# Attention masks as 64-row products beside the scores they mask, in a fused attention, expert and convolution kernel

## The chip, the core and the metric

The kernel runs on one core of one Trainium2 chip. Time is device time in microseconds (us) of one execution; less is better. Before the change three runs took 479.0, 471.89 and 477.14 us, the median is 477.14 us. Names of engines: PE multiplies matrices, PEld is its weight load, DVE, ACT and POOL work element by element, SP issues the transfers.

## The reference

Three layers follow each other on a batch of 4. The first is attention with 8 heads of width 64 over 512 local and 32 global tokens; a local query sees the global keys and the local keys at most 32 positions away. The second has 4 experts, each a causal attention over the 544 tokens with a head width of 64, of which every token takes two by its gate. The third is a projection to 1024 channels, a convolution of width 3 along the tokens, a gate and a projection back.

```python
mask = np.abs(pos[:, None] - pos[None, :]) <= 32
s_ll = np.where(mask, scale * q_l @ k_l.T, -1e9)          # local attention
a_l = softmax(concat([scale * q_l @ k_g.T, s_ll]))
x = concat([softmax(scale * q_g @ k_all.T) @ v_all, a_l @ concat([v_g, v_l])])
for e in range(4):                                         # experts
    scores = np.where(causal, -1e9, scale * (x @ wq[e]) @ (x @ wk[e]).T)
    out += gate[e] * (softmax(scores) @ (x @ wv[e]) @ wo[e])
h = relu(out @ w_in)                                       # convolution and gate
y = (h * sigmoid(conv3(h))) @ w_out
```

## The kernel before

The program is recorded as a list of operations and put in order by a planner (class `Recorder`, lines 154 to 314): each operation has a due number, set by `due(...)`, and a cost by engine, and each engine takes the ready operation with the lowest due number whose tiles have a free buffer. The due numbers come from the table in lines 37 to 40. Every instruction is emitted in line 314, so the profile names all of them L314, and one tells them apart by the names of their tiles. A float32 product of full accuracy is made of three products of split operands (names ending in h and l).

Phase A (one batch, four pairs of heads; `phase_a`) computes local attention. `scores_l` takes two score tiles `s`, one for each head of a pair. Sixteen blocks of 32 queries by 128 keys go into each: block 4i + j lies on PSUM partitions 32j to 32j + 31. The two heads lie on the two halves of the partitions, so a score product (`s<-rk,rq`) uses 64 rows and 32 columns of PE's array. The mask is added by products too: for each head and each j the product of 32 columns of an identity (`identb`) with the table `lmask` (`s<-lmask,identb`, 512 columns wide, bfloat16), over all 128 rows. DVE then takes the maximum (`ml`), ACT the exponential (`Pa`). `scores_g` does the 32 global queries (`Pg`, `PGT`), `pv_l` and `pv_g` multiply with the values (`t<-vr,p` and `t<-PGT,vr`).

Phase B (`phase_b`) makes queries and keys of four experts (`s<-xh,wqkh` and the like), values (`s<-wvh,xh`) and the gates. For each of 2 pairs of experts and 4 blocks of 128 queries, `scores` runs six score products over 64 rows, three for each expert (`s<-kh,qh`, `s<-kl,qh`, `s<-kh,qlo`), the two experts on the two halves of the rows. Two products of the full identity with `causal` follow over all 128 rows (`s<-cm,identb`, 128 by 128). `trans` (`t<-ident,w`) and `pv` (`t<-p,vB`) use the result; `last` handles the last 32 queries.

Phase C (`phase_c`) multiplies with the folded weight (`s<-oh,wfh`), does the convolution on ACT and DVE, and multiplies with the output weight (`s<-gh,wuh`). The fold (`s<-gl,oh`), and the decoding of 64-bit weights on DVE and POOL that fold and output weight need, run in the first 200 us beside phases A and B of the first two batches.

SP loads in one queue in the planner's order: the mask tables (`w<-in_cmask_dram`), keys and queries (`rk`, `rq`), values (`vr`), weights.

Of the kernel before, what the change touches and what calls it, by code (L numbers as in the profile page):

```python
# [8 lines left out]
F32 = mybir.dt.float32  # L9
F32R = mybir.dt.float32r  # L10
BF = mybir.dt.bfloat16
I32 = mybir.dt.int32
# [11 lines left out]
BIG = 1e9  # L24
# [9 lines left out]

AHEAD = 1

PERIOD, A_AT, A_STEP, LOAD_AHEAD = 54.5, 0.0, 5.0, 21.5
B_AT, LAST, ITEMS, ITEM_STEP = 29.0, 54.0, 9.0, 2.45
C_AT, C_HALF, C_PROJ = 80.0, 41.0, 36.5
FOLD, FOLD_STEP, WOUT, WOUT_STEP = 12.0, 1.45, 75.0, 2.0  # L40


def local_mask():

    import numpy as np
    m = np.zeros((128, 4, 128), np.float32)
    q = np.arange(32)[:, None]
    for n in range(NG_):
        for c, kb in enumerate(KEYS[FIRST[n]:FIRST[n] + 4]):
            if kb != "g":  # L50
                t = 32 * kb + np.arange(32)[None, :]
                ok = (abs(q + 32 * n - t) <= 32) & (t >= 0) & (t < SL)
                m[32 * (n % 4):32 * (n % 4) + 32, n // 4, 32 * c:32 * c + 32] = np.where(ok, 0.0, -BIG)
    return m
# [282 lines left out]
def width(v):  # L337
    n = 1
    for k in v.shape[1:]:
        n *= k  # L340
    return n


def cost_pe(node, method, out, args, kw):
    us = 0.0 if node.calls else 0.03
    node.lag = 0.25
    if method == "transpose":
        return us + 0.11
    lhs, N = args[1], width(out)
    K, M = lhs.shape[0], width(lhs)  # L350
    if lhs.dt == F32R:
        one = max(0.107, N / 2400 + 0.013)
        return us + (one if K > 64 else one / 2)
    if lhs.dt == BF:
        return us + (0.06 if M == 32 else max(0.107, N / 2400 + 0.013))
    if K == 64:
        return us + max(0.03, N / 2400 if N > 128 else 0.0)
    if M == 32 and N == 64:
        return us + 0.03
    if N >= 256 or N == 64:  # L360
        return us + 4 * N / 2400 + 0.03
    return us + (0.066 if N <= 32 else 0.115)
# [24 lines left out]
def body(ctx, tc, kq, vA, w_gate, wqk, wv, woT, w_in, conv_w, w_out, cmask, out):  # L387
    nc = tc.nc
    NB = kq.shape[0]
    rec = Recorder()  # L390
    pe, act = rec.engine("PE", nc.tensor, cost_pe), rec.engine("ACT", nc.scalar, cost_act)
    dve, pool = rec.engine("DVE", nc.vector, cost_dve), rec.engine("POOL", nc.gpsimd, cost_pool)
    sp = rec.engine("SP", nc.sync, cost_dma)
# [4 lines left out]
    def T(shape, dt, name, bufs=1):  # L398
        return rec.tile(sb, shape, dt, name, bufs)

    def due(us):
        rec.due = us
# [7 lines left out]
    def W2():  # L410
        return T([128, 512], F32, "w2", 4)
# [52 lines left out]
    identb = T([128, 128], BF, "identb")  # L464
    dve.tensor_copy(identb, ident)

    cm = T([128, 160], BF, "cm")
    causal, last_mask = cm[:, :128], cm[:, 128:160]
    trif = T([128, 4, 4], F32, "trif")

    due(-30)
# [17 lines left out]
    def projections_gen():  # L489
        due(-5)  # L490
        w = W2()
        sp.dma_start(w[:, :160], cmask[:, 512:672])
        dve.tensor_copy(cm, w[:, :160])
        sp.dma_start(trif, cmask[:, 672:688].rearrange("p (a b) -> p a b", a=4))
        w = W2()
        pool.memset(w[:, :256], 0.0)
        for t in (ql, qll):
            scale_pool(t, w[:, :256].rearrange("p (a b) -> p a b", a=2), 1.0)
        for c in range(4):
            due(4 + 2 * c)  # L500
            w = W2()
            sp.dma_start(w, wqk[128 * c:128 * c + 128])
            split(wqkh[:, c], wqkl[:, c], w, act)
        for c in range(4):
            due(14 + 2 * c)
            w = W2()
            sp.dma_start(w[:, :256], wv[128 * c:128 * c + 128])
            sp.dma_start(w[:, 256:260], w_gate[128 * c:128 * c + 128])
            split(wvh[:, c], wvl[:, c], w[:, :260], act)
# [28 lines left out]

    def conv_load():
        due(FOLD)  # L540
        rawc = T([128, 24, 2], I32, "rawc")
        sp.dma_start(rawc.rearrange("p a b -> p (a b)"), conv_w.bitcast(I32))
        decode(rawc, 24, cw.rearrange("p k f -> p (k f)"))

# [10 lines left out]
    NPA, NPT = 2, 4  # L555
    NRK, NRQ, NXQ = 2, 2, 1
    xs = {}
    lmask = T([128, 512], BF, "lmask")


    Pg = T([128, 6, 128], F32, "Pg")
# [43 lines left out]
    def scores_l(k, q):  # L605

        t = [PS(4, 128) for _ in range(2)]
        rows = [slice(64 * y, 64 * y + 64) for y in range(2)]
        P = [T([128, 4, 128], F32, "Pa", NPA) for _ in range(2)]
        rec.claim(*P)  # L610
        with rec.group():
            for y in range(2):
                for j in range(4):
                    r = slice(32 * j, 32 * j + 32)
                    pe.matmul(t[y][r].rearrange("p i c -> p (i c)"), identb[:, r], lmask, start=True, stop=False)
            for i in range(4):
                for j in range(4):
                    g = 4 * i + j
                    for y in range(2):
                        pe.matmul(t[y][32 * j:32 * j + 32, i], q[rows[y], 32 * g:32 * g + 32],  # L620
                                  k[rows[y], 32 * FIRST[g]:32 * FIRST[g] + 128], start=False, stop=(i == 3))

        ml = T([128, 4, 4, 2], F32, "ml", 3)
        for y in range(2):
            dve.tensor_reduce(ml[:, 0, :, y], t[y], axis=AX.X, op=ALU.max, negate=True)
            dve.tensor_scalar(ml[:, 0, :, y], ml[:, 0, :, y], SCALE, None, op0=ALU.mult)
            for i in range(4):
                act.activation(P[y][:, i], t[y][:, i], AF.Exp, bias=ml[:, 0, i, y:y + 1], scale=SCALE,
                               accum_out=ml[:, 1, i, y:y + 1])
        dve.tensor_scalar(ml[:, 2], ml[:, 1], EPS, None, op0=ALU.add)  # L630
        dve.reciprocal(ml[:, 3], ml[:, 2])
        return P, ml[:, 3]
# [60 lines left out]

    def consts_a():
        due(-25)
        w = W2()
        sp.dma_start(w, cmask[:, :512])
        dve.tensor_copy(lmask, w)

    def phase_a(b):  # L700
        for c in range(0, 4, 2):
# [28 lines left out]
    def phase_b(b):  # L730
# [3 lines left out]
        for t, (dh, dl, sc) in enumerate(((qh, qlo, 0.125), (kh, kl, 1.0))):  # L734
            for p in range(2):
                m = slice(256 * t + 128 * p, 256 * t + 128 * p + 128)
# [15 lines left out]
        for i in range(5):  # L752
            r = 128 if i < 4 else 32
# [4 lines left out]
            with rec.group():  # L758
              for c in range(4):
                for xa, wa in ((xh, wvh), (xh, wvl), (xl, wvh)):  # L760
                    pe.matmul(acc[:r, :260], xa[c][:, 128 * i:128 * i + r], wa[:, c, :], start=(n == 0),
                              stop=(n == 11))
# [31 lines left out]
        for e in range(4):  # L794
            r0, p = 64 * (e % 2), e // 2
# [7 lines left out]
        for z in range(2):  # L803
            w = keys[z].stop - keys[z].start
            t = PS(512)[:, :w]
# [20 lines left out]
        t = PO(4, 128)  # L826
# [5 lines left out]
        t = PO(4, 128)  # L832
# [5 lines left out]
        def scores(p, i):  # L838

            st = T([128, 8], F32, "stB", 4)  # L840
            w = 128 * (i + 1)
            qi = slice(128 * i, 128 * i + 128)
            t = [PS(512) for _ in range(2)]
            PB = [W2() for _ in range(2)]
            rec.claim(*PB)
            with rec.group():
                for n, (a, k) in enumerate(((qh, kh), (qh, kl), (qlo, kh))):
                    for y in range(2):
                        rows = slice(64 * y, 64 * y + 64)
                        pe.matmul(t[y][:, :w], a[rows, p, qi], k[rows, p, :w], start=(n == 0), stop=False)  # L850
                for y in range(2):
                    pe.matmul(t[y][:, w - 128:w], identb, causal, start=False, stop=True)
            for y in range(2):
                dve.tensor_reduce(st[:, y:y + 1], t[y][:, :w], axis=AX.X, op=ALU.max, negate=True)
                P = PB[y]
                act.activation(P[:, :w], t[y][:, :w], AF.Exp, bias=st[:, y:y + 1],
                               accum_out=st[:, 2 + y:3 + y])
            dve.tensor_scalar(st[:, 4:6], st[:, 2:4], EPS, None, op0=ALU.add)
            dve.reciprocal(st[:, 4:6], st[:, 4:6])
            for y in range(2):  # L860
                pool.tensor_scalar(PB[y][:, :w], PB[y][:, :w], st[:, 4 + y:5 + y],
                                   gate[:, i, 2 * p + y:2 * p + y + 1], op0=ALU.mult, op1=ALU.mult)
            live[p, i] = PB
# [132 lines left out]
def host_layout(inputs):  # L996
    import numpy as np
    c = np.ascontiguousarray
# [5 lines left out]
    for n in range(NG_):  # L1004
        for j, kb in enumerate(KEYS[FIRST[n]:FIRST[n] + 4]):
            for y in range(2):
                if kb == "g":
                    vA[:, :, 32 * j:32 * j + 32, n, y] = vg[:, y::2]
                elif 0 <= kb < NG_:
                    vA[:, :, 32 * j:32 * j + 32, n, y] = vl[:, y::2, 32 * kb:32 * kb + 32]  # L1010
    cm = np.zeros((128, 688), np.float32)
    cm[:, :512] = local_mask().reshape(128, 512)
    p = np.arange(128)
    cm[:, 512:640] = np.where(p[None, :] > p[:, None], -BIG, 0.0)
    cm[:, 640:672] = np.where(p[None, :32] > (p[:, None] % 32), -BIG, 0.0)
    cm[:, 672:688] = np.where(np.arange(4)[None, :] < np.arange(4)[:, None], 1.0, 0.0).reshape(1, 16)
    bits = lambda w: c(w).view(np.int64)
    hw = lambda w: np.concatenate(list(w), axis=1)

# [36 lines left out]
```

## Time and profile before

| | |
|---|---|
| Median of three runs | 477.14 us (471.89 to 479.0) |
| Profiled execution | 474.14 us, its span 472.3 us |
| PE busy | 440.8 us, 93% of the span |
| DVE, ACT, POOL busy | 72%, 65%, 36% |
| Read from memory | 38.40 MB |

Matmuls are pipelined: on this page a matmul of 272 columns shows 0.29 us of duration while the next one starts 0.125 us later. What one costs is therefore read as the distance between two starts, and a busy PE is not a PE at its peak. In a name such as `64*32 64x128` the first pair is rows and columns of the array in use, the second what streams through it.

### The profile page before, as it was taken

The numbers are of one execution on the slowest core, as the hardware profiler recorded it, in microseconds if no ns is written. First come the engines' busy times: TensorE is split into PE (matmuls) and PEld (weight loads), VectorE is DVE, ScalarE is ACT, GpSimd is POOL, SyncE is SP. The second block draws the span as 40 slices with busy tenths as digits, with TensorE's granted clock in tenths as the row PEclk, the third lists the DMA queues.
The fourth block names the chain that finished last, engine by engine and source line by source line (L and its number), as shares of the span: only waits on it lengthen the run. The fifth ranks groups of instructions, "written<-read, shape, count | busy, mean of one in ns | idle before, by whom it ended". The sixth has DMA issues, their size and how long they took to land.

```text
span 472.3 us, 14650 instructions
## 1 busy us (share of the span) xinstructions
PE 440.8 (93%) x5768; PEld 382.9 (81%) x5768; DVE 338.6 (72%) x970; ACT 305.8 (65%) x1017; POOL 168.9 (36%) x285
## 2 busy tenths in 40 slices
PE   5688799999989998999999999999999999999996
PEld 2556699765779886779879987799899997989996
DVE  3586677989987998899528746688448386957770
ACT  3677574667667776778448846586568454837771
POOL 2066879864786637950000011330000033400000
PEclk9989899999989999999999999999999999999999
DMA  8977612443561124320134004300100000000101
GB/s 291 303 239 257 218 46 81 145 152 122 171 214 47 44 72 159 96 98 15 58 129 147 14 7 154 104 14 14 63 21 3 0 26 25 13 26 1 48 25 47
DMA packets 21348, 43.79 MB, mean 93 GB/s; under 512 B 3104, under 2 KB 8352, under 8 KB 21280
## 3 DMA queue, kind: packets, MB, share of 16 engines
q1 hardware_dynamic: 21280, 42.86, 27.1%
q8 instruction: 45, 0.74, 0.7%
q14 instruction: 23, 0.19, 0.1%
HBM read 38.40 MB, written 4.46 MB: 91 GB/s over the span
## 4 chain that ended last, share of the span: by engine, by line
PE 59%; DVE 16%; POOL 9%; ACT 6%; issue 5%; DMA 3%; SPq 0%; DVEq 0%; POOLq 0%; ACTq 0%
PE s L314 43%; PE t L314 16%; DVE cv L314 6%; POOL cv L314 4%; POOL hb L314 3%; DVE hb L314 2%; DVE gl L314 2%; DVE stB L314 2%; DVE ml L314 2%; ACT cv L314 2%; DMA vr<-in_vA_dram 1%; ACT hb L314 1%; DMA w<-in_w_gate_dram 1%; POOL gl L314 1%; DMA rq<-in_kq_dram 1%
## 5 line engine op out<-in xcount | busy, mean ns | idle before, releaser
L314 PE MATMUL s<-gh,wuh 128*128 128x272 f32 x256 | 78.4, 306 | 0.4 <-ACT gh L314 0.3
L314 POOL TENSOR_SCALAR w<-w,stB,gate 128x128 f32<-128x128 f32 (+3 forms) x64 | 42.9, 681 | 91.5 <-DVE glast L314 44.2
L314 DVE SCALAR_TENSOR_TENSOR cv<-hb,cw,cv 128x272 f32<-128x272 f32 x128 | 64.4, 515 | 15.1 <-ACT cv L314 12.4
L314 PE MATMUL s<-gl,wuh 128*128 128x272 f32 x256 | 74.1, 289 | 0.6 <-DVE gl L314 0.5
L314 PE MATMUL s<-gh,wul 128*128 128x272 f32 x256 | 73.8, 288 | 0.0
L314 ACT ACTIVATE Pa<-s,ml 128x128 f32<-128x128 f32 x128 | 45.7, 368 | 29.4 <-DVE ml L314 25.8
L314 PEld LDWEIGHTS s<-gh,wuh 128*128 128x128 f32 x256 | 48.4, 189 | 2.2 <-ACT gh L314 1.1
L314 PEld LDWEIGHTS s<-gl,wuh 128*128 128x128 f32 x256 | 48.3, 189 | 1.3 <-DVE gl L314 1.3
L314 PEld LDWEIGHTS s<-gh,wul 128*128 128x128 f32 x256 | 48.3, 189 | 0.0
L314 ACT ACTIVATE w<-s,stB 128x128 f32<-128x128 f32 (+3 forms) x64 | 33.5, 527 | 16.4 <-DVE stB L314 16.0
L314 POOL TENSOR_SCALAR hb<-hb 128x256 f32<-128x256 f32 (+1 forms) x33 | 36.7, 1112 | 11.1 <-ACT hb L314 11.0
L314 PE MATMUL s<-oh,wfh 128*128 128x274 f32 x128 | 38.2, 299 | 1.2 <-DVE kl L314 0.8
L314 PE MATMUL s<-xh,wqkh 128*128 128x272 f32 x128 | 38.5, 301 | 0.0
L314 PE MATMUL s<-xh,wqkl 128*128 128x272 f32 x128 | 38.2, 299 | 0.0
L314 PE MATMUL s<-xl,wqkh 128*128 128x272 f32 x128 | 38.0, 297 | 0.0
L314 DVE COPY p<-t 128x128 f32<-128x128 f32 (+3 forms) x64 | 29.9, 484 | 10.9 <-PE t L314 10.8
L314 PE MATMUL s<-oh,wfl 128*128 128x274 f32 x128 | 37.2, 290 | 0.0
L314 PE MATMUL s<-ol,wfh 128*128 128x274 f32 x128 | 37.1, 290 | 0.0
L314 POOL TENSOR_TENSOR cv<-cv,hb 128x256 f32<-128x256 f32 (+1 forms) x33 | 25.1, 760 | 33.6 <-DVE hb L314 32.3
L314 ACT ACTIVATE cv<-cv 128x272 f32<-128x272 f32 x64 | 27.4, 429 | 13.5 <-DVE cv L314 12.7
L314 PE MATMUL t<-ident,w 128*128 128x128 f32 x176 | 30.3, 282 | 5.1 <-POOL w L314 2.7
L314 DVE TENSOR_REDUCE stB<-s 128x1 f32<-128x128 f32 (+3 forms) x64 | 29.8, 483 | 6.6 <-PE s L314 6.2
(152 smaller groups left out, 1257.3 us busy)
## 6 DMA issues: line engine op xcount, KB each, us to landing
vr<-in_vA_dram SPq DMA_DIRECT2D x32, 512.0 KB, 5.6
rk<-in_kq_dram SPq DMA_DIRECT2D x16, 384.0 KB, 3.8
rq<-in_kq_dram SPq DMA_DIRECT2D x16, 272.0 KB, 4.2
out_dram<-y SPq DMA_DIRECT2D x32, 136.0 KB, 1.7
w<-in_w_in_dram SPq DMA_DIRECT2D x16, 256.0 KB, 3.0
w<-in_w_out_dram SPq DMA_DIRECT2D x16, 256.0 KB, 2.6
w<-in_wqk_dram SPq DMA_DIRECT2D x4, 256.0 KB, 5.7
w<-in_woT_dram SPq DMA_DIRECT2D x2, 256.0 KB, 6.8
```

The lines of the kernel that those rows point to most:

```text
L314: getattr(n.eng.nc, method)(*map(real, args), **{k: real(v) for k, v in kw.items()})
```

## The change

The local mask goes through 64 rows. Its table is stored twice, once on each half of the partitions, as two pieces of 512 columns for queries 0 to 63 and 64 to 127 of a tile; each head uses the rows of its own half, the same array tile as its scores. There are still eight products of 512 columns.

The causal mask is cut in two as well. Each half of the mask's rows stands on both halves of the partitions. For each expert two products over its own 64 rows replace one over 128: the first takes the mask for queries 0 to 63 and is 128 columns wide, the second for queries 64 to 127 and is 64 wide. Where the query half is not the expert's own half of the partitions, the identity with swapped halves (`swapb`) takes the place of `identb`. Two products become four.

The constants grow from 688 to 1456 columns and are loaded in three pieces in place of two. `ml` has 2 buffers in place of 3, `rawc` shares the buffers of `w64`. The table of the planner's due numbers is new, so operations move on all engines.

```diff
-PERIOD, A_AT, A_STEP, LOAD_AHEAD = 54.5, 0.0, 5.0, 21.5
-B_AT, LAST, ITEMS, ITEM_STEP = 29.0, 54.0, 9.0, 2.45
...
+PERIOD, A_AT, A_STEP, LOAD_AHEAD = 54.0, 0.0, 6.0, 1.5
+B_AT, LAST, ITEMS, ITEM_STEP = 29.0, 54.0, 9.0, 2.35
...
-        return us + (0.06 if M == 32 else max(0.107, N / 2400 + 0.013))
+        return us + (0.06 if K == 64 else max(0.107, N / 2400 + 0.013))
...
-        sp.dma_start(w[:, :160], cmask[:, 512:672])
-        dve.tensor_copy(cm, w[:, :160])
...
+        sp.dma_start(w[:, :416], cmask[:, 1024:1440])
+        dve.tensor_copy(cm, w[:, :416])
...
-        rawc = T([128, 24, 2], I32, "rawc")
+        rawc = T([128, 512], F32, "w64", 2).bitcast(I32)[:, :48].rearrange("p (a b) -> p a b", b=2)
...
-                    pe.matmul(t[y][r].rearrange("p i c -> p (i c)"), identb[:, r], lmask, start=True, stop=False)
+                    one = 64 * y + 32 * (j % 2)
+                    pe.matmul(t[y][r].rearrange("p i c -> p (i c)"), identb[rows[y], one:one + 32],
+                              lmask[rows[y], j // 2], start=True, stop=False)
...
-        ml = T([128, 4, 4, 2], F32, "ml", 3)
+        ml = T([128, 4, 4, 2], F32, "ml", 2)
...
-        w = W2()
-        sp.dma_start(w, cmask[:, :512])
-        dve.tensor_copy(lmask, w)
+        for h in range(2):
+            w = W2()
+            sp.dma_start(w, cmask[:, 512 * h:512 * h + 512])
+            dve.tensor_copy(lmask[:, h], w)
...
-                for y in range(2):
-                    pe.matmul(t[y][:, w - 128:w], identb, causal, start=False, stop=True)
+
+                for h in range(2):
+                    for y in range(2):
+                        rows = slice(64 * y, 64 * y + 64)
+                        pe.matmul(t[y][:, w - 128 + 64 * h:w], (identb if h == y else swapb)[rows],
+                                  causal[rows, h, 64 * h:], start=False, stop=(h == 1))
...
+    twice = lambda m: np.stack([np.concatenate([h, h]) for h in (m[:64], m[64:])], axis=1).reshape(128, -1)
```

Two places show what moves. The first is the head of SP's queue. Before, the first keys and queries (`rk`, `rq`) stood behind one piece of constants:

```order
L314 DMA w_70<-in_cmask_dram 128x512
L314 DMA rk<-in_kq_dram 128x768
L314 DMA rq<-in_kq_dram 128x544
L314 DMA rk<-in_kq_dram 128x768
L314 DMA rq<-in_kq_dram 128x544
L314 DMA vr<-in_vA_dram 128x1024 x3
L314 DMA w_101<-in_cmask_dram 128x160
L314 DMA trif<-in_cmask_dram 128x16
```

Now:

```order
L314 DMA w_70<-in_cmask_dram 128x512
L314 DMA w_77<-in_cmask_dram 128x512
L314 DMA w_81<-in_cmask_dram 128x416
L314 DMA trif<-in_cmask_dram 128x16
L314 DMA rk<-in_kq_dram 128x768
L314 DMA rq<-in_kq_dram 128x544
L314 DMA rk<-in_kq_dram 128x768
L314 DMA rq<-in_kq_dram 128x544
```

All constants now stand ahead of the first keys.

The second is PE at the second item of the first batch's phase B: six score products and the causal mask behind them. Before:

```order
L314 MATMUL s<-kh,qh 128x128 x2
L314 MATMUL s<-kl,qh 128x128 x2
L314 MATMUL s<-kh,qlo 128x128 x2
L314 LDWEIGHTS identb
L314 MATMUL s<-cm,identb 128x128
L314 LDWEIGHTS identb
L314 MATMUL s<-cm,identb 128x128
L314 MATMUL s<-wvh,xh 32x260
```

The same kind of group now (`s<-cm` is the product with `swapb`, which lies in `cm`):

```order
L314 MATMUL s<-kh,qh 128x128 x2
L314 MATMUL s<-kl,qh 128x128 x2
L314 MATMUL s<-kh,qlo 128x128 x2
L314 LDWEIGHTS identb
L314 MATMUL s<-cm,identb 128x128
L314 LDWEIGHTS cm
L314 MATMUL s<-cm 128x128
L314 LDWEIGHTS cm
L314 MATMUL s<-cm 128x64
L314 LDWEIGHTS identb
L314 MATMUL s<-cm,identb 128x64
L314 MATMUL s<-oh,wfh 128x274
```

Four loads and four products stand where two and two stood.

## Rows read from the trace of the kernel before

**Rows 1.** The page, its head and part 1: busy time of each engine.

```profile
span 472.3 us, 14650 instructions
PE 440.8 (93%) x5768; PEld 382.9 (81%) x5768; DVE 338.6 (72%) x970; ACT 305.8 (65%) x1017; POOL 168.9 (36%) x285
```

**Rows 2.** Busy time by stretch; PEclk is the granted clock as a share.

```profile
core 0: us, PE busy (x) PEld busy (x) DVE busy (x) ACT busy (x) POOL busy (x), PEclk, DMA share, GB/s
0.00:60.00 60.00, 44.60 (x875) 32.06 (x876) 36.01 (x105) 37.00 (x135) 29.08 (x43) 0.94 0.77 258
60.00:200.00 140.00, 130.97 (x1891) 109.64 (x1889) 122.25 (x361) 95.38 (x336) 100.93 (x139) 0.99 0.34 113
200.00:450.00 250.00, 246.56 (x2865) 223.12 (x2864) 171.61 (x485) 163.01 (x522) 38.77 (x103) 1.00 0.14 46
450.00:472.30 22.30, 18.71 (x145) 18.07 (x143) 8.77 (x21) 10.38 (x27) 0.10 (x1) 1.00 0.11 38
```

**Rows 3.** Waits of PE from 60 us on, longest in total first.

```profile
PE t L314 <- POOL w L314: 2.7, 4, 1.5
PE s L314 <- POOL gl L314: 2.2, 4, 0.9
PE t L314 <- DVE ol L314: 2.0, 4, 0.7
```

**Rows 4.** Timeline of PE at a local mask: start, duration, operation.

```profile
194.24 0.44 PE L314 MATMUL t<-ident,w 128*128 128x128 f32 x2
194.61 0.61 PE L314 MATMUL s<-lmask,identb 128*32 128x512 bf16 x8
195.15 1.16 PE L314 MATMUL s<-rk,rq 64*32 64x128 f32 x64
196.24 0.33 PE L314 MATMUL t<-ident,w 128*128 128x128 f32 x1
```

**Rows 5.** Timeline of PE, a causal mask with a 128-row stage behind it.

```profile
207.15 0.39 PE L314 MATMUL s<-kl,qh 64*128 64x512 f32 x2
207.38 0.40 PE L314 MATMUL s<-kh,qlo 64*128 64x512 f32 x2
207.71 0.29 PE L314 MATMUL s<-cm,identb 128*128 128x128 bf16 x2
207.81 0.37 PE L314 MATMUL s<-oh,wfh 128*128 128x274 f32 x1
208.02 0.29 PE L314 MATMUL s<-ol,wfh 128*128 128x274 f32 x1
208.15 0.29 PE L314 MATMUL s<-oh,wfl 128*128 128x274 f32 x1
```

**Rows 6.** Timeline of PE, a causal mask with column tiles behind it.

```profile
393.00 0.34 PE L314 MATMUL s<-kl,qh 64*128 64x384 f32 x2
393.17 0.34 PE L314 MATMUL s<-kh,qlo 64*128 64x384 f32 x2
393.44 0.28 PE L314 MATMUL s<-cm,identb 128*128 128x128 bf16 x2
393.65 0.66 PE L314 MATMUL t<-p,vB 128*64 128x128 f32 x8
```

**Rows 7.** Timeline of PE, 64 small products of 128 rows, then 128x128.

```profile
294.75 1.17 PE L314 MATMUL t<-vr,p 128*32 128x64 f32 x64
295.86 0.39 PE L314 MATMUL s<-gh,wuh 128*128 128x272 f32 x1
296.08 0.29 PE L314 MATMUL s<-gl,wuh 128*128 128x272 f32 x1
```

**Rows 8.** Timeline of PE, 64-row pairs, then full products of 32 columns.

```profile
82.17 0.27 PE L314 MATMUL s<-kl,qh 64*128 64x128 f32 x2
82.28 0.27 PE L314 MATMUL s<-kh,qlo 64*128 64x128 f32 x2
...
211.08 0.26 PE L314 MATMUL s<-kh,qlast_l 128*128 128x32 f32 x1
211.19 0.26 PE L314 MATMUL s<-kh,qlast_h 128*128 128x32 f32 x1
```

**Rows 9.** Timelines of SP and PE at the start.

```profile
0.72 0.37 SPq L314 DMA_DIRECT2D w<-in_cmask_dram  x1
1.14 0.42 SPq L314 DMA_DIRECT2D rk<-in_kq_dram  x1
...
3.73 1.05 PE L314 MATMUL s<-lmask,identb 128*32 128x512 bf16 x8 [3.73 <-DVE lmask L314]
5.93 3.78 PE L314 MATMUL s<-rk,rq 64*32 64x128 f32 x80 [1.16 <-DMA rq<-in_kq_dram]
```

More of the change, by code (lines that the diff above doesn't have):

```diff
@@ L35 @@
 AHEAD = 1
-PERIOD, A_AT, A_STEP, LOAD_AHEAD = 54.5, 0.0, 5.0, 21.5
-B_AT, LAST, ITEMS, ITEM_STEP = 29.0, 54.0, 9.0, 2.45
-C_AT, C_HALF, C_PROJ = 80.0, 41.0, 36.5
-FOLD, FOLD_STEP, WOUT, WOUT_STEP = 12.0, 1.45, 75.0, 2.0
+PERIOD, A_AT, A_STEP, LOAD_AHEAD = 54.0, 0.0, 6.0, 1.5
+B_AT, LAST, ITEMS, ITEM_STEP = 29.0, 54.0, 9.0, 2.35
+C_AT, C_HALF, C_PROJ = 80.0, 42.0, 43.5
+FOLD, FOLD_STEP, WOUT, WOUT_STEP = 12.0, 1.25, 75.0, 2.0
 def local_mask():
@@ L465, in body @@
     dve.tensor_copy(identb, ident)
-    cm = T([128, 160], BF, "cm")
-    causal, last_mask = cm[:, :128], cm[:, 128:160]
+    cm = T([128, 416], BF, "cm")
+    causal, swapb, last_mask = cm[:, :256].rearrange("p (h k) -> p h k", h=2), cm[:, 256:384], cm[:, 384:416]
     trif = T([128, 4, 4], F32, "trif")
@@ L491, in projections_gen @@
         w = W2()
-        sp.dma_start(w[:, :160], cmask[:, 512:672])
-        dve.tensor_copy(cm, w[:, :160])
-        sp.dma_start(trif, cmask[:, 672:688].rearrange("p (a b) -> p a b", a=4))
+        sp.dma_start(w[:, :416], cmask[:, 1024:1440])
+        dve.tensor_copy(cm, w[:, :416])
+        sp.dma_start(trif, cmask[:, 1440:1456].rearrange("p (a b) -> p a b", a=4))
         w = W2()
@@ L557, in body @@
     xs = {}
-    lmask = T([128, 512], BF, "lmask")
+    lmask = T([128, 2, 512], BF, "lmask")
     Pg = T([128, 6, 128], F32, "Pg")
@@ L1010, in host_layout @@
                     vA[:, :, 32 * j:32 * j + 32, n, y] = vl[:, y::2, 32 * kb:32 * kb + 32]
-    cm = np.zeros((128, 688), np.float32)
-    cm[:, :512] = local_mask().reshape(128, 512)
+    twice = lambda m: np.stack([np.concatenate([h, h]) for h in (m[:64], m[64:])], axis=1).reshape(128, -1)
+    cm = np.zeros((128, 1456), np.float32)
+    cm[:, :1024] = twice(local_mask().reshape(128, 512))
     p = np.arange(128)
-    cm[:, 512:640] = np.where(p[None, :] > p[:, None], -BIG, 0.0)
-    cm[:, 640:672] = np.where(p[None, :32] > (p[:, None] % 32), -BIG, 0.0)
-    cm[:, 672:688] = np.where(np.arange(4)[None, :] < np.arange(4)[:, None], 1.0, 0.0).reshape(1, 16)
+    cm[:, 1024:1280] = twice(np.where(p[None, :] > p[:, None], -BIG, 0.0))
+    cm[:, 1280:1408] = np.where(p[None, :] == (p[:, None] + 64) % 128, 1.0, 0.0)
+    cm[:, 1408:1440] = np.where(p[None, :32] > (p[:, None] % 32), -BIG, 0.0)
+    cm[:, 1440:1456] = np.where(np.arange(4)[None, :] < np.arange(4)[:, None], 1.0, 0.0).reshape(1, 16)
     bits = lambda w: c(w).view(np.int64)
```

## The prediction

> **What bounds the kernel now.** I read the page's busy shares first: PE is at 93%, the next engine at 72% [rows 1]. A share over the whole span hides stages, so the table by stretch comes second [rows 2]. Up to 60 us PE is busy for 44.60 us only, while transfers run at 258 GB/s and 77%: that stretch belongs to loading and to the chain behind it. From 60 to 200 us PE is busy for 130.97 of 140 us, so it idles 9.0 us; DVE is at 122.25, close behind. From 200 to 450 us PE idles 250 - 246.56 = 3.4 us: it is the bound, and time taken from it is time gained. The waits say the same [rows 3]: from 60 us on the longest sum is 2.7 us in four waits for POOL. What PE spends per step has then to be read in the timeline, as distances from start to start.
>
> **The price of a switch.** Products over 64 rows and over 128 rows don't overlap each other. With 512 columns a pair over 64 rows takes 207.38 - 207.15 = 0.23 us; the next pair of the same length is followed by the 128-row mask after 207.71 - 207.38 = 0.33 us [rows 5]. So going from 64 to 128 rows costs 0.10 us. With 384 columns it is 0.27 against 0.17, the same 0.10 [rows 6].
>
> **Local mask.** From the first mask product to the first score product pass 195.15 - 194.61 = 0.54 us [rows 4]: two rounds of four column tiles (2 x 0.23 by rows 5, for 512 columns) and a switch of about 0.1. Now each head's four products go to the array tiles of its own rows. That eight such tiles run side by side is seen in the score products behind the mask: 64 of 128 columns take 196.24 - 195.15 = 1.09 us, while 64 of half that width, over 128 rows and so in four tiles, take 295.86 - 294.75 = 1.11 us [rows 4, 7]. One round of 0.23 us and some 0.02 for starting eight remain, and no switch before the scores, since both use 64 rows by 32 columns: 0.25 us in place of 0.54, a gain of 0.29. The switch into the mask from what precedes it stays. There are 16 such groups. Eleven start after 60 us, where PE counts: 11 x 0.29 = 3.2 us. Five start before: the first is covered by the wait for `rq`, since PE has done its masks and idles 1.16 us until 5.93 [rows 9]; for the other four I take half, 0.6, since PE idles a quarter of that stretch. Together 3.8 us. The ends: 16 x 0.29 = 4.6 if all count, and 16 x 0.08 = 1.3 if the two heads don't run side by side and only the switch goes (0.54 - 0.46).
>
> **Causal mask.** 32 groups. With column tiles behind, the two mask products with the switch out take 393.65 - 393.44 = 0.21 us; less 0.10 for that switch they cost 0.11 [rows 6]. Now there is no switch ahead of them, and two pairs follow each other. A pair over 64 rows has not been seen in bfloat16; in float32 a pair of half loads goes by in 82.28 - 82.17 = 0.11 us, the same as one full load, 211.19 - 211.08 = 0.11 [rows 8]. So I price a pair as a full product: 2 x 0.055 = 0.11 us, 0.12 with the start of four. Then comes the switch that the group before had ahead of its masks, 0.10. What this gains depends on the follower:
> - Column tiles (`t<-p,vB`): 0.48 - 0.17 = 0.31 us beyond the score pair before [rows 6], now 0.12 + 0.10 = 0.22: a gain of 0.09. In the new order 11 of the 32 groups have a follower that is no 128-row stage in full columns (ten `t<-p,vB`, one local mask), before it were 13.
> - A 128-row stage (21 of 32): 207.81 - 207.38 - 0.23 = 0.20 us beyond the pair, now 0.22. Its second product then comes 0.21 us after the first [rows 5], behind a switch 0.22 [rows 7]. So a loss of 0.02 to 0.03.
>
> 11 x 0.09 - 21 x 0.025 = 0.5 us of gain: the switch is mostly moved from ahead of the mask to behind it. The upper end is 32 x 0.09 = 2.9. The lower end, halves that load one after the other, is the rival below.
>
> **A rule against it.** The Trainium skill (TensorE: Matmul & The Clock Gate, section on LDWEIGHTS) says that a weight load is paid by its columns, and that fewer rows save nothing. The rows agree for one load and show the two halves passing together in float32. If they did not, four loads at that page's 107 ns in place of two would raise my sum by 32 x 0.21 = 6.8 us, an estimate from that page.
>
> **The start.** The first `rk` was issued at 1.14 us behind one piece of constants [rows 9]; now it is behind four transfers. Three more at 0.42 us or a little over (the distance from 0.72 to 1.14) make 1.3 us; the bytes ahead of it grow by 256 + 208 + 8 = 472 KB, 1.8 us at 258 GB/s [rows 2]. So the scores of 5.93 us start 1.3 to 1.8 us later. Some is given back, since the causal constants no longer come between the first values and the weights, and PE's chain has waits in that stretch: between 0 and 1.8 us, I take 0.9. DVE's larger casts lie in the same wait.
>
> **The order.** Off the masks, counting changes of array tiling between neighbours gives about as many as before, so I cost this at nothing on PE. Loads of later batches stand at like places in SP's queue, a place or two later: what frees them is a buffer, and the due number changes little. `ml` with 2 buffers keeps local scores from running further ahead; the work of phase C covers that, and if it is missing, PE waits for `t<-vr,p` chains as in the first 60 us. The larger decode in the buffers of `w64` is one small transfer. What the new table does to PE's 12.4 us of waits between 60 and 450 us I can't read from an order; zero is taken, 6 either way kept for the range.
>
> **Sum.** 3.8 + 0.5 - 0.9 = 3.4 us less than the profiled 474.14 us: 470.7. The median before lies 3.0 us over that execution, so the median would be 477.14 - 3.4 = **473.7 us**.
>
> **Rivals.**
> - *Waits go too* (faster). The new table closes half of the 12.4 us of waits: 473.7 - 6.2 = 467.5, with all local gains 467 and less. For it: the waits are single ones on POOL and DVE [rows 3], which a shift of an operation can fill. Against: nothing in the rows says that it would rather close than open them. 462 to 470 us, chance 0.27.
> - *Absorbed* (no change). From 60 to 200 us DVE at 87% paces PE [rows 2]; only the five local groups and half of the causal gain after 200 us count: 5 x 0.29 + 0.25 = 1.7, less 0.9 at the start, 476.3 us. Against: PE idles 6% there. 475 to 479, chance 0.15.
> - *Half loads queue* (slower). In the causal groups the bfloat16 halves load one after the other: four at 0.055 us are 0.22 in place of 0.11, 32 x 0.11 = 3.5 us more; at the 0.11 us of a full float32 load [rows 8] 0.44, 32 x 0.33 = 10.6 more. So 477 to 484, about 481 in the middle. It decides from 3.4 / 32 = 0.11 us per group on. For it: more loads for the same mask. Against: the pairs in float32. The rule above would give 473.7 + 6.8 = 480.5. Chance 0.13.
> - The forecast, 471 to 476 us: chance 0.45.
>
> **How the numbers follow.** About 2% is what a measurement of this kernel can tell from no change: its runs spread from 471.89 to 479.0. Faster by over 2% means under 467.6: somewhat over half of the first rival, 0.15. Slower means over 486.7, the far end of half loads plus a bad order: 0.03. Within 2%: 0.82. The range 464 to 480 leaves out the best part of the first rival (0.08) and the far end of the last (0.07), some order that opens waits included.
>
> **What will show it.** From the first local mask product to the first score product 0.25 us (0.46 if the heads don't run side by side). Behind the last `s<-kh,qlo` pair of 512 columns the first mask product after 0.23 us in place of 0.33, the follower 0.22 us later; 0.33 or more says that the halves queue. The first `s<-rk,rq` at 7.2 to 7.7 us. The forecast is wrong if PE's idle time from 60 to 450 us moves from 12.4 us by more than 6, or if that before 60 us grows by more than 2.

## The result, and the profile after

The changed kernel takes 470.91 us (median of 20 runs, 465.8 to 475.56), the kernel before 475.38 us in the same series (20 runs). The ratio, taken from the faster executions of each, is 0.9877, with a 95% interval from 0.9847 to 0.9907: 5.9 us less, where the medians lie 4.5 us apart. The forecast was 3.4 us less. The profiled execution took 466.55 us with a span of 464.8; the one before 474.14. Executions of one program spread over some 2%, and much of that goes with the granted clock: one slope fitted to all kernels of this document gives 0.29 us more for each 0.001 of granted clock less. So single executions are compared at like granted clocks.

The head of the page and the busy times by stretch, in the columns of [rows 2]:

```profile
span 464.8 us, 14768 instructions
PE 434.1 (93%) x5832; PEld 383.0 (82%) x5832; DVE 339.8 (73%) x971; ACT 304.0 (65%) x1017; POOL 168.6 (36%) x285
...
0.00:60.00 60.00, 44.37 (x882) 32.88 (x883) 38.98 (x108) 37.22 (x135) 29.16 (x44) 0.94 0.79 264
60.00:200.00 140.00, 130.89 (x1946) 112.05 (x1946) 125.64 (x369) 97.11 (x345) 104.94 (x143) 1.00 0.37 120
200.00:450.00 250.00, 247.65 (x2925) 227.53 (x2923) 171.75 (x488) 165.64 (x528) 34.52 (x100) 1.00 0.13 44
```

PE is busy 6.7 us less than before (440.8 in [rows 1]), while the other engines do what they did. Part of that is clock: a second trace of the changed kernel, at a mean granted clock of 0.985 and not 0.992, has PE busy for 436.2 us. Its idle time from 60 to 450 us is 9.1 + 2.35 = 11.5 us, against 12.4 [rows 2]. So the span's 7.5 us are mostly shorter work on PE. By name, though, the waits are new ones (total, times, longest, in us):

```profile
PE s L314 <- POOL gl L314: 1.7, 2, 1.3
PE t L314 <- POOL w L314: 1.5, 3, 0.9
PE t L314 <- DVE p L314: 1.4, 3, 0.8
PE t L314 <- issue: 1.3, 1, 1.3
```

In [rows 3] POOL's `w` stood at 2.7 and DVE's `ol` at 2.0; those shrank or went. The 1.3 us of "issue", in which PE waited for nothing that the profile names, is taken up below.

The timeline of PE at a local mask, which answers to [rows 4]:

```profile
102.56 0.44 PE L314 MATMUL t<-ident,w 128*128 128x128 f32 x2
102.93 0.41 PE L314 MATMUL s<-lmask,identb 64*32 64x512 bf16 x8
103.15 1.37 PE L314 MATMUL s<-rk,rq 64*32 64x128 f32 x61
```

All eight products are out in one round: 0.226 us to the first score in the unrounded records of 13 of the 16 groups, where it was 0.546. The score products behind it, first to last, take 0.863 in place of 0.887. A group costs 0.34 us less.

The timeline of PE at two causal masks, one with column tiles behind it, which answers to [rows 6], one with a 128-row stage, which answers to [rows 5]:

```profile
98.37 0.28 PE L314 MATMUL s<-kl,qh 64*128 64x256 f32 x2
98.49 0.28 PE L314 MATMUL s<-kh,qlo 64*128 64x256 f32 x2
98.61 0.23 PE L314 MATMUL s<-cm,identb 64*128 64x128 bf16 x1
98.61 0.25 PE L314 MATMUL s<-cm 64*128 64x128 bf16 x2
98.68 0.19 PE L314 MATMUL s<-cm,identb 64*128 64x64 bf16 x1
98.80 0.44 PE L314 MATMUL t<-p,vB 128*64 128x128 f32 x4
...
393.56 0.40 PE L314 MATMUL s<-kh,qlo 64*128 64x512 f32 x2
393.80 0.23 PE L314 MATMUL s<-cm,identb 64*128 64x128 bf16 x1
...
393.99 0.39 PE L314 MATMUL s<-gh,wuh 128*128 128x272 f32 x1
394.22 0.29 PE L314 MATMUL s<-gl,wuh 128*128 128x272 f32 x1
```

The pair of 256 columns ahead of the mask passes in 98.61 - 98.49 = 0.12 us, as the pair before it: no switch there. The two heads' halves start together (the second row at 98.61 holds one product of each of the two pairs), the next pair 0.07 us later, and the follower 0.12 us after that. Mask start to follower is 0.19 us. At 393 us it is 0.24 for 512 columns and 0.19 again; the follower's second product comes 0.23 us after its first.

The timelines of SP and PE at the start, which answer to [rows 9]:

```profile
0.72 1.33 SPq L314 DMA_DIRECT2D w<-in_cmask_dram  x3
2.09 0.43 SPq L314 DMA_DIRECT2D trif<-in_cmask_dram  x1
2.57 0.43 SPq L314 DMA_DIRECT2D rk<-in_kq_dram  x1
...
8.16 4.23 PE L314 MATMUL s<-rk,rq 64*32 64x128 f32 x76 [2.85 <-DMA rq<-in_kq_dram]
```

`rk` goes out 1.43 us later, and the first scores start 2.23 us later.

### The profile page after: what moved, and what is told of

Same layout as the page of the kernel before. It is cut to its first block, busy times and chain, and to the rows that moved or that the text cites. A ratio compares the mean times of both kernels' runs of the same rounds, so it can differ in the third digit from the quotient of the medians.

```text
span 464.8 us, 14768 instructions
## 1 busy us (share of the span) xinstructions
PE 434.1 (93%) x5832; PEld 383.0 (82%) x5832; DVE 339.8 (73%) x971; ACT 304.0 (65%) x1017; POOL 168.6 (36%) x285
## 4 chain that ended last, share of the span: by engine, by line
PE 69%; DVE 10%; POOL 6%; DMA 5%; ACT 4%; issue 3%; SPq 1%; ACTq 0%; POOLq 0%; DVEq 0%
PE s L314 51%; PE t L314 19%; DVE cv L314 4%; DMA vr<-in_vA_dram 2%; POOL cv L314 2%; POOL hb L314 2%; SPq L314 1%; DVE ml L314 1%; DMA w<-in_w_in_dram 1%; DVE hb L314 1%; DMA rq<-in_kq_dram 1%; DVE p L314 1%; DVE gl L314 1%; DMA rk<-in_kq_dram 1%; POOL gl L314 1%
## 5 line engine op out<-in xcount | busy, mean ns | idle before, releaser
L314 DVE SCALAR_TENSOR_TENSOR cv<-hb,cw,cv 128x272 f32<-128x272 f32 x128 | 65.9, 526 | 12.3 <-ACT cv L314 10.3
L314 ACT ACTIVATE w<-s,stB 128x128 f32<-128x128 f32 (+3 forms) x64 | 33.3, 524 | 10.5 <-DVE stB L314 9.8
L314 PE MATMUL s<-xh,wqkh 128*128 128x272 f32 x128 | 37.2, 291 | 0.1
L314 PE MATMUL s<-xh,wqkl 128*128 128x272 f32 x128 | 36.9, 288 | 0.0
L314 PE MATMUL s<-xl,wqkh 128*128 128x272 f32 x128 | 36.8, 288 | 0.0
L314 PE MATMUL s<-rk,rq 64*32 64x128 f32 (+2 forms) x1152 | 32.4, 313 | 2.8 <-DMA rq<-in_kq_dram 2.8
L314 DVE TENSOR_TENSOR gl<-cv,gh 128x272 fp32r<-128x272 f32 x64 | 28.3, 457 | 8.3 <-ACT gh L314 7.7
L314 ACT ACTIVATE cv<-hb,cw 128x272 f32<-128x272 f32 x64 | 33.0, 519 | 0.7
```

The lines of the kernel that those rows point to most:

```text
L314: getattr(n.eng.nc, method)(*map(real, args), **{k: real(v) for k, v in kw.items()})
```

## Experiments

The theory: shorter masks are the gain, and the new order and the later start cost or give little. The rivals: the new order is the gain; the masks' gain needs the new order; and, found on the way, the later start eats the gain in one order and not in the other. Ratios are to the kernel before, run on the same chip in turn, with 95% intervals.

**Old masks in the new order.** `both128` keeps the changed kernel's order, constants and staging, and puts both masks back over 128 rows; `local128` and `causal128` put one of them back. The planner's costs are held so that the order does not move. The edits of the first:

```
-pe.matmul(t[y][r]..., identb[rows[y], one:one + 32], lmask[rows[y], j // 2], ...)
+pe.matmul(t[y][r]..., identb[:, r], lmask[:, 0], ...)
...
-for h in range(2):
-    for y in range(2):
-        pe.matmul(t[y][:, w - 128 + 64 * h:w], (identb if h == y else swapb)[rows], causal[rows, h, 64 * h:], ...)
+for y in range(2):
+    pe.matmul(t[y][:, w - 128:w], identb, causal[:, 0], ...)
```

> The changed kernel's order and tables of due numbers, every instruction in the same place, with both masks over 128 rows as before (the same stored tables, whose first piece is the whole mask). Theory A (the masks made the gain): about 5 to 6 us slower than the changed kernel, that is the time of before, ratio to before 0.997 to 1.003; local groups again 0.54 us from mask to scores. Theory B (the new order made the gain): within 1.5 us of the changed kernel, ratio about 0.988.

> The changed kernel, same order, only the local mask over 128 rows again. Theory A: 16 groups longer by 0.546 - 0.226 = 0.32 us, of which 11 lie after 60 us: 3.5 to 5.1 us slower than the changed kernel, ratio to before 0.995 to 0.999. Theory B: under 1.5 us slower.

> The changed kernel, same order, only the causal mask over 128 rows again. Theory A, by followers: 11 groups with other tiles behind longer by 0.13 us, 21 with 128-row stages the same to 0.01: about 1.2 us slower than the changed kernel, ratio to before about 0.990. If the causal part gains as much per group everywhere, 32 x 0.13 = 4 us slower.

Measured: `both128` 0.9969 (0.9935 to 1.0004), 472.37 us; `local128` 0.9912 (0.9878 to 0.9947); `causal128` 0.9877 (0.9837 to 0.9918). In this order the two masks are worth 0.9969 - 0.9877, or 4.4 us. `causal128` came near its forecast; `local128` fell between its two accounts. How the 4.4 us divide isn't settled by the ratios: the local mask is worth 1.7 us (`local128` against the changed kernel) or 4.4 (`both128` against `causal128`). In the traces the last product comes 1.80 us earlier than in `both128` with the local one alone and 2.38 with the causal one alone, but there the clock decides: from 90 to 110 us it was 0.74 in `causal128` and 0.91 in `both128`, and the lead of `causal128` fell from 3.9 us near 90 us to 1.7 near 120. At one clock (below) the local mask is worth 2.8 us and the causal one 0.5, which can't be told from none. The stretches of `both128`:

```profile
60.00:200.00 140.00, 132.53 (x1845) 112.05 (x1844) 122.58 (x361) 95.92 (x340) 102.68 (x139) 0.99 0.35 113
200.00:450.00 250.00, 248.00 (x2940) 224.88 (x2940) 172.34 (x490) 164.40 (x525) 38.25 (x104) 1.00 0.15 48
```

PE idles 7.5 + 2.0 = 9.5 us there, 2.9 less than before [rows 2]: the new order by itself closes waits. Its ratio's interval just holds 1; at one clock (below) the gain is clear of noise.

**The order's two halves.** `newtable` is the kernel before with the four lines of due numbers of the changed one, and `oldtable` the changed kernel with the old four lines.

```
-PERIOD, A_AT, A_STEP, LOAD_AHEAD = 54.0, 0.0, 6.0, 1.5
+PERIOD, A_AT, A_STEP, LOAD_AHEAD = 54.5, 0.0, 5.0, 21.5
...
```

> The kernel before, with the changed kernel's table of due numbers and nothing else. Theory A (masks about 4 us, order about 2 us of the 5.9 us, from the run with both masks over 128 rows in the changed order at 0.997): about 2 us faster than before, ratio 0.993 to 0.999. Rival (the table does nothing by itself): ratio 1.000 within 0.002, or slower, since the table was set for other costs.

> The changed kernel with the table of due numbers of before; masks over 64 rows, larger constants, 2 buffers of ml. Theory A: the masks' 4 us remain and the order's 2 us go: ratio to before 0.990 to 0.994, PE waits after 60 us back near 12 us. Rival: the masks alone make all of it, ratio 0.988.

Measured: `newtable` 1.0024 (0.9993 to 1.0055), 475.92 us; `oldtable` 1.0309 (1.0258 to 1.0359), 489.17 us. The table gives the old code nothing that shows, as the rival had it, and the new code loses 20 us without it, which neither account expected. The waits of PE from 60 to 450 us in `oldtable`:

```profile
PE t L314 <- DVE xl L314: 4.7, 5, 1.3
PE t L314 <- issue: 3.1, 2, 1.9
PE t L314 <- DVE ol L314: 3.0, 4, 1.2
```

PE idles 25.5 us in that stretch. A planned order is a term of its own, of 4% here (1.0309 against 0.9877), between two kernels whose products are the same.

**New masks in the old order.** `masks_in_before` is the missing corner: the kernel before with the 64-row masks and their tables, while the planner sees the old costs, so that every engine keeps its old order. What differs besides the products is one more piece of constants at the start (staged in `vB`), a wider cast, and the convolution weights' staging, also in `vB`. `after_again` is the changed kernel once more, in the same series.

```
+pe.matmul(... 64-row products of the change ...)
-return us + (0.06 if M == 32 else max(0.107, N / 2400 + 0.013))
+return us + (0.06 if M == 32 else 0.0535)
+rec.nodes[-1].cost = 128 * 160 * 4 / 300e3
```

> The kernel before with both masks in 64 rows and the tables for them, but with every engine's order as in the kernel before (the products of the masks, two constant pieces and where the convolution weights are staged are all that differs). Theory A (the masks carry the gain, whatever the order): 16 local groups x 0.32 us and 32 causal groups x about 0.04 us leave PE, some 6 us, of which part comes back as waits; ratio 0.988 to 0.992, busy time of PE about 434 us, idle time between 60 and 450 us 12 to 14 us. Rival B (the masks' gain needs the new order, since in the old one the engines behind pace PE): ratio 0.995 to 1.000, PE's busy time down by the same 6 us, but its idle time between 60 and 450 us up from 12.4 to 16 us or more.

> The changed kernel itself once more, on the same chip and in the same rounds as the one above, so that the two can be set side by side: ratio 0.985 to 0.991, first scores at about 8.2 us, PE idle between 60 and 450 us about 11.5 us. Theory A expects the kernel above within 0.004 of it, rival B 0.006 or more above it.

Measured: `masks_in_before` 0.9986 (0.9952 to 1.0021), 473.47 us; `after_again` 0.9919 (0.9871 to 0.9968), 472.86 us, a little above its range. So the four corners are:

| | masks over 128 rows | masks over 64 rows |
|---|---|---|
| old order | 1 | 0.9986 |
| new order | 0.9969 | 0.9877; again 0.9919 |

By the ratio rival B's range was met. Its sign was not: PE idles 10.5 + 4.4 = 14.9 us from 60 to 450 us, between theory A's 12 to 14 and rival B's 16 or more. The stretches of `masks_in_before`:

```profile
PE 434.4 (92%) x5832; PEld 383.6 (81%) x5832; DVE 339.7 (72%) x971; ACT 305.8 (65%) x1017; POOL 169.1 (36%) x285
...
0.00:60.00 60.00, 41.86 (x870) 31.13 (x871) 36.74 (x104) 36.57 (x133) 28.50 (x43) 0.91 0.80 258
60.00:200.00 140.00, 129.51 (x1923) 110.75 (x1923) 122.36 (x362) 96.05 (x337) 101.62 (x139) 0.99 0.36 116
200.00:450.00 250.00, 245.63 (x2909) 224.91 (x2910) 172.82 (x488) 164.08 (x526) 38.96 (x105) 1.00 0.14 46
```

PE's work fell by 6.4 us, and its idle time (span less busy) rose from 31.5 to 471.2 - 434.4 = 36.8: 5.3 of the 6.4 came back as waits, half of them before 60 us (18.1 idle for 15.4). The first scores start at 7.33 us there, not at 5.93. That could be the cause, so the last run gives the old order its old start: `masks_old_start` loads the second piece of the local table behind the first values and takes the first local mask alone over 128 rows.

```
+a, m = (identb[:, r], lmask[:, 0]) if whole else (identb[rows[y], one:one + 32], lmask[rows[y], (j // 2) ^ y])
+pe.matmul(t[y][r]..., a, m, start=True, stop=False)
```

> As masks_in_before (the order of the kernel before, 64-row masks), with the start of the kernel before: the second piece of the local mask's table is loaded behind the first values and the other constants and cast behind them, and the first local group alone takes its mask over 128 rows. This sets the two accounts of masks_in_before apart, whose first scores came 1.40 us late and whose last product 1.27 us early. Theory C (the masks give about as much in the old order as in the new one, 2.7 us, and the later start took 1.4 of it): first scores at 5.9 to 6.1 us, the last product 2.2 to 3 us earlier than in the kernel before, ratio 0.993 to 0.996. Rival B (the old order absorbs the masks' gain, and a start brought back is absorbed as well): first scores as early, but the last product still 1.0 to 1.6 us earlier only, ratio 0.996 to 1.000.

Measured: 0.9963 (0.9917 to 1.001), 471.31 us; the interval takes in both accounts. Since the order of PE is the same in each pair below, the start of the same product can be set side by side (us; the second less the first; the product is `s<-gl,ol` or `s<-gl,oh` near 68 us, `s<-xl,wqkh` near 144 us and `s<-gh,wul` at the end):

| product | before, `masks_in_before` | | before, `masks_old_start` | | `both128`, `after_again` | |
|---|---|---|---|---|---|---|
| first scores | 5.93, 7.33 | +1.40 | 5.93, 6.12 | +0.19 | 8.28, 7.94 | -0.34 |
| near 68 us | 67.31, 68.09 | +0.78 | 67.31, 66.39 | -0.93 | 68.92, 66.10 | -2.82 |
| near 144 us | 144.26, 145.16 | +0.90 | 144.26, 144.20 | -0.06 | 144.94, 141.60 | -3.34 |
| last | 468.82, 467.55 | -1.27 | 468.82, 465.80 | -3.02 | 465.81, 462.14 | -3.68 |

By the last product the masks give 3.02 us in the old order and 3.68 in the new; against the changed kernel's first trace, at a granted clock of 0.992, it is 4.67. These are single traces, and the two of the changed kernel itself end 1.00 us apart. The mean granted clocks are near each other (0.989, 0.986 and 0.985 in the old order; 0.985 twice in the new), but the lower of the two levels, 1.2 GHz in place of 2.4, falls in other places. Two stretches of the kernel before, then of `masks_old_start`, in the columns of [rows 2]:

```profile
90.00:110.00 20.00, 17.63 (x333) 12.64 (x326) 18.55 (x61) 13.74 (x56) 12.48 (x19) 1.00 0.60 195
130.00:150.00 20.00, 18.47 (x300) 16.74 (x298) 15.21 (x45) 12.94 (x46) 14.73 (x21) 0.91 0.44 141
...
90.00:110.00 20.00, 17.62 (x267) 12.43 (x267) 16.22 (x56) 12.06 (x50) 11.91 (x18) 0.83 0.49 159
130.00:150.00 20.00, 17.95 (x307) 16.12 (x306) 17.44 (x46) 13.73 (x48) 15.61 (x22) 1.00 0.43 141
```

So that the lead of `masks_old_start` is gone near 144 us says nothing of its order. `masks_in_before` has the clocks of the kernel before in both stretches, and there the old order does gain nothing from 68 to 144 us. From 144 us on the granted clock is 1.00 in all these traces, and from there to the last product the masks gain 2.2 and 3.0 us in the old order, and 0.3 in the new (0.6 with the first trace). Rival B, with 1.0 to 1.6 us at the end, does not fit 3.02; theory C does. That the old order pays for the later start to the very end is not shown. The two ends lie 3.02 - 1.27 = 1.75 us apart, but `masks_in_before` had caught up by 25 us, at a higher clock, and fell behind again near 38 us, where PE waits 2.46 us for `vr` and 1.10 us in `masks_old_start`.

PE's waits for POOL's `w` from 60 to 145 us are 2.8 us in `masks_in_before` and were 2.3 before:

```profile
PE t L314 <- POOL w L314: 2.8, 3, 2.1
PE s L314 <- POOL gl L314: 2.3, 4, 0.9
```

The executions behind each ratio also had different clocks. Brought to a granted clock of 0.985 by the slope named above, and with the kernel before taken over all series, they give an estimate of what each kernel takes less than the kernel before (us, with 95% intervals):

| kernel | us less |
|---|---|
| `both128`: new order, masks over 128 rows | 2.3 (1.5 to 3.1) |
| `local128`: new order, causal mask alone over 64 rows | 2.8 (1.8 to 3.8) |
| `causal128`: new order, local mask alone over 64 rows | 5.1 (4.0 to 6.2) |
| the changed kernel, and again | 5.7 (5.0 to 6.4), 5.1 (4.1 to 6.0) |
| `masks_in_before`: old order, later start | 2.0 (1.2 to 2.8) |
| `masks_old_start`: old order, old start | 3.2 (2.3 to 4.0) |

At one clock, then, the masks are worth 2.0 us in the old order, 3.2 with its old start, and 3.4 or 2.8 in the new: about the same in either. The new order alone is worth 2.3. `masks_in_before` comes to 0.996 and so stays within rival B's numbers, but its ground falls: the masks gain in the old order too, and what sets that kernel apart from the changed one is mostly the order's own 2.3 us. `masks_old_start` comes to 0.993, in theory C's range and outside rival B's. The 1.2 us between the two starts have an interval from 0.1 to 2.3.

**The start.** `kqfirst` and `kqfirst2` issue the causal constants behind the first values, or behind the first keys and queries; the first also casts them late on DVE. The edit, in `kqfirst`:

```
+for n, after in ((sp[2], sp[9]), (sp[3], sp[2]), (cast, dve[18])):
+    order.remove(n)
+    order.insert(order.index(after) + 1, n)
```

> The changed kernel with the causal constants (load, cast, trif) behind the first keys, queries and values; all else in the same order. If the late start lasts: first scores at about 6.3 us in place of 8.16 and 1 to 1.9 us faster than the changed kernel, ratio to before about 0.985. If the first 60 us absorb it: first scores earlier as well, the time the same within 0.5 us.

> As the run with the causal constants behind the first keys, but the cast of these constants stands early on DVE, so that the buffer is free before SP needs it for the output weight's transfer. If the late start costs time: SP no longer waits at 8.25 us, first scores at about 6.7 us, 1 to 1.5 us faster than the changed kernel, ratio about 0.985. If the first 60 us absorb it: 0.988.

Measured: `kqfirst` 0.9937 (0.9895 to 0.9978); `kqfirst2` 0.987 (0.9819 to 0.992). In `kqfirst` the first scores start at 6.72 us, but SP then stands at a weight load from 8.25 to 15.6 us, because the cast, at 17.83 us, holds one `w` buffer, and the next comes free only with DVE's `wqkl` at 14.48 us:

```profile
8.25 7.33 SPq L321 DMA_DIRECT2D w<-in_woT_dram  x2
15.63 0.46 SPq L321 DMA_DIRECT2D w<-in_conv_w_dram  x1
16.14 0.42 SPq L321 DMA_DIRECT2D w<-in_w_in_dram  x1
16.66 0.38 SPq L321 DMA_DIRECT2D rk<-in_kq_dram  x1
```

It moved a wait from the start to the next keys, and tells nothing of the start's price. `kqfirst2` does: its first scores come 1.93 us earlier than the changed kernel's,

```profile
6.23 2.73 PE L321 MATMUL s<-rk,rq 64*32 64x128 f32 x66 [0.97 <-DMA rq<-in_kq_dram]
```

and the ratio is the same, 0.987 and 0.9877. By the `gl,ol` products near 55 us the lead over the changed kernel is down to 1.17 us, and near 71 us to 0.3. Against the second trace of the changed kernel, whose granted clock is the same up to 60 us (0.91) and from 90 to 110 us (0.91), the lead is 1.70 us at the first scores, gone near 68 us and 0.01 at the last product. In these traces the new order absorbs the later start. By the executions at one clock `kqfirst2` is 0.8 us faster than the changed kernel, with an interval from -0.5 to 2.1, so a part of it may be paid.

**The order of the causal halves.** `youter` puts both products of one expert ahead of both of the other in the program (`for y` outside `for h`).

> The changed kernel, same order, the four causal products sorted by expert and not by query half, so that products that follow each other use the same rows twice and the two experts meet only in the middle. If side-by-side halves matter: a group grows from 0.066 us between pairs by 0.06 to 0.13 us, 2 to 4 us in all, ratio to before 0.992 to 0.996. If not: same as the changed kernel, 0.988.

Measured: 0.9913 (0.9878 to 0.9947), an interval that overlaps the changed kernel's. In its trace pairs start 0.07 us apart and the follower 0.12 us later, as above; its wait for "issue" (next) was 1.9 us. No difference by the order of the halves is shown, and the trace says why: the products start in the same order as in the changed kernel. At 98.98 us the third of the program, on the other half of the rows, starts 3 ns behind the first, and the second 66 ns behind it. Each half takes its own products in turn.

**The wait for "issue".** The timeline of PE at that wait in the changed kernel:

```profile
132.65 0.41 PE L314 MATMUL s<-lmask,identb 64*32 64x512 bf16 x8
132.88 1.13 PE L314 MATMUL s<-rk,rq 64*32 64x128 f32 x64
133.94 0.66 PE L314 MATMUL t<-ident,w 128*128 128x128 f32 x4
134.53 1.14 PE L314 MATMUL t<-vr,p 128*32 128x64 f32 x62
136.99 0.27 PE L314 MATMUL t<-vr,p 128*32 128x64 f32 x2 [1.32 <-issue]
```

The last two products of one run of 64 wait, though they need what the 62 needed. In all nine traces of the new order (the changed kernel twice and the seven made from it with its table) a wait of 0.40 to 1.90 us stands behind the same number of recorded instructions of PE and its weight load, 4,033, whichever product comes next: in `both128`, with fewer mask products ahead, it is the fifteenth of `t<-PGT,vr`, after 0.40 us. There are others: `both128` and `causal128` also wait 0.28 us behind 3,009 instructions, which is 1,024 earlier, `newtable` 0.59 and `masks_old_start` 0.17 us behind 4,034, and `kqfirst2` 1.02 us at 39 us. `pad121` puts four float32 products of the identity, which the mask overwrites, ahead of the one mask at 132.65 us (the trace records two products for each):

```
+for i in range(4):
+    pe.matmul(first[:, i % 4], ident, ident, start=True, stop=True)
```

> The changed kernel with four extra 128x128 float32 products of the identity with itself, which the mask products then overwrite, ahead of one local mask only, the group at 132.65 us of its trace; nothing else is changed. Behind that group stands PE's wait of 1.32 us in the middle of a run of `t<-vr,p` products, for nothing that the profile names, in front of the 4,033rd instruction that the trace records on PE. Theory A (the wait is for the program itself: PE comes to its next piece of instructions too early): the extra 0.6 to 1.2 us of products cost nothing or little, the wait shrinks by what they take, to 0.1 to 0.7 us, and it stands some 8 to 16 instructions earlier in the run, still at the 4,033rd. Rival B (the wait belongs to the data or buffers of those `t<-vr,p` products): it stays at 1.3 us in front of the same two last products, and all steps behind come 0.6 to 1.2 us later. In time: 0.986 to 0.993 for both, the difference lies below what the rounds tell apart, so the trace decides.

Measured, the same stretch of `pad121`:

```profile
135.59 1.06 PE L317 MATMUL s<-ident 128*128 128x128 f32 x8
136.58 0.41 PE L320 MATMUL s<-lmask,identb 64*32 64x512 bf16 x8
...
138.46 1.08 PE L320 MATMUL t<-vr,p 128*32 128x64 f32 x54
139.97 0.43 PE L320 MATMUL t<-vr,p 128*32 128x64 f32 x10 [0.43 <-issue]
```

The products added 0.99 us, the wait fell from 1.32 to 0.43 and moved to the 55th product: eight products more ahead, with their loads, so again behind 4,033 instructions. What follows came 0.1 us later, not 1 us. The ratio is 0.9832 (0.9788 to 0.9876); no difference to the changed kernel is shown. So the wait goes with the place in the program and not with data: PE comes to this place too early, and with more work ahead of it, as here and in `both128`, it waits less. That it waits for its next instructions is inferred from that; no row names it. No version run here is shown to beat the changed kernel.

## Why the prediction was right, and where it was not

*Local mask.* Right in mechanism, and near in size on PE: 0.25 us from mask to scores was forecast, 0.226 came, and 16 x 0.34 = 5.5 us left PE where I had 16 x 0.29 = 4.6 at most. In time the local mask is worth 2.8 us at one clock (`causal128` less `both128`, 1.5 to 4.1), where I had 3.8.

*Causal mask.* The switch ahead of it is gone and stands behind it, as forecast. A pair costs what a full product costs, as I had it, but that is 0.066 us and not 0.055: the two full products of the kernel before start 0.066 us apart as well. Mask start to follower is 0.19 us, not 0.22. A 128-row follower's second product is 0.23 us behind the first, so such groups gain nothing: from the last score pair to that second product it was 0.64 us [rows 5] and is 394.22 - 393.56 = 0.66. The ones with column tiles gain 0.31 - 0.19 = 0.12 each [rows 6]. That is 11 x 0.12 - 21 x 0.02 = 0.9 us on PE where I had 0.5.

Together I let the masks count for 3.8 + 0.5 = 4.3 us. By ratios they gave 4.4 in the new order, or 0.9969 - 0.9919 = 2.4 with the second series; by the last product 3.0 in the old and 3.7 to 4.7 in the new. At one clock they gave 2.0 and 3.2 in the old, 3.4 and 2.8 in the new. Of the 6.4 us that left PE the rest came back as waits. That the size is near my 4.3 is in part luck, for I had put the gain in another place: 3.2 of the 3.8 us behind 60 us, "where PE counts". In the new order (`both128` against `after_again`) the lead grows by 2.5 us up to 68 us, 1.2 of it between 56 and 60 us, where the clock of `both128` alone was low (0.72 from 56 to 62 us against 1.00), and from 144 us to the end, where seven of the local groups stand, by 0.3. There PE waits in the changed kernel 1.2 us for POOL's `w` in place of 0.7, and 0.6 for `vr` in place of none that shows. So a PE that is hardly ever idle did not pass its savings on in full.

*The rule.* The two halves of a pair start together, and the four loads and products of a group are through in 0.07 + 0.12 us. The Trainium skill (TensorE: Matmul & The Clock Gate, section on LDWEIGHTS) charges each load by its columns, whatever its rows. This trace agrees for one load in float32 (0.11 us [rows 8]). In bfloat16 a full product with its load passed in 0.066 us already before the change, less than the 0.107 that I took from there, and two loads into different row halves pass together. So the 6.8 us by that rule did not come. *Half loads queue* fell with it: its sign was 0.33 us or more from mask to follower.

*The start.* This step was mis-sized. The first scores came 2.2 us later, more than the 1.3 to 1.8 of my sum; I charged 0.9 us. In the old order 1.75 us lie between the two starts by the last product and 1.2 at one clock (`masks_in_before` against `masks_old_start`); the new one pays nothing that shows in the traces (`kqfirst2`). What PE waits for next in that stretch decides, and I had taken half.

*The order.* This step failed: it was taken as worth nothing. With the old masks and the later start the new order ends 472.3 - 469.4 = 2.9 us earlier, by the ratio 0.9969, or 1.5 us, with an interval that just touches none. At one clock it is 2.3 us, from 1.5 to 3.1. The later start is inside that, so order and start together, for which I had 0.9 us of loss, were a gain of 2.3. That is what the forecast was short of: 4.3 - 0.9 = 3.4 us forecast, and 3.4 for the masks with 2.3 for the order make the 5.7 that came at one clock.

*The rivals.* *Waits go too* was half right: 12.4 us of waits fell to 9.5 by the order, and the shorter masks brought them back to 11.5, 0.9 of it as the longer wait for the program (0.40 to 1.32). *Absorbed* describes `masks_in_before` from 68 to 144 us, where the wait that grew most was one for POOL and not for DVE, and not the changed kernel as a whole.

What stays open: which moves of the new order close the waits and hide the start, and how much of the start the old order pays. The orders differ in hundreds of places, and no single one was tried.

## What to carry to other kernels

A shorter product is priced well from distances in the timeline; what decides the total is whether the loads it needs come at the start of the chain, and which order hides them. Hold the order and change the products, then the reverse, and compare the start of the same product in both traces: that shows where a gain is made and lost. Look at the granted clock of each stretch first, for where it falls can move the end by more than the effect in question (1.00 us between two traces of the changed kernel). And compare many executions at one clock: in this way the masks' gain in the old order came out, which the ratio 0.9986 had hidden.

## What was not expected of the hardware

- Two products of 64 rows in bfloat16, each with its own load, follow the next two after 0.066 us, as long as one full product takes, and eight tiles of 64 by 32 with 512 columns pass in 0.226 us.
- The two halves of the rows each keep their own order: at 108.61 us of the changed kernel, where the second expert's products come late, the third product of the group starts 0.066 us behind the first and the second one 0.154 us behind it.
- PE can wait at a place of its program, whatever product stands there: 0.40 to 1.90 us behind the same count of instructions in nine traces. In the changed kernel the 138 products ahead of it, most of them short, stand in 3.0 us (132.65 to 135.67).
- The same four lines of due numbers moved one program by 20 us and another by 1 (an interval that holds none), with the same products in each.
